# Loading padded inputs in one transfer over 112 partitions, earlier and into five buffers, and letting the state update go through PSUM

## The chip, the cores and the metric

The kernel runs on one core of a Trainium2 chip. The metric is the device time in microseconds of one execution, lower is better. A profile of one execution gives every instruction's start and duration; times in it count from the start of its span.

## What is computed

Three layers follow each other: a gated linear attention over 768 steps, a mixture of 8 experts in which each token goes to its best expert, and a mixture of 4 experts in which each token goes to all of them. The reference, cut to its core:

```
# attention, B=4, H=8, S=768, D=48
for t in range(S):
    state = alpha[:, :, t, :, None] * state + np.einsum('bhd,bhe->bhde', k[:, :, t], v[:, :, t])
    y[:, :, t] = np.einsum('bhd,bhde->bhe', q[:, :, t], state)
...
x = attn_out.transpose(0, 2, 1, 3).reshape(B * S, H * D)
# first mixture, 3072 tokens of 384, 8 experts of 1024
expert_idx = np.argmax(logits, axis=1)
for e in range(E):
    out[mask] = gate_w[mask, None] * (np.maximum(x[mask] @ w1[e], 0.0) @ w2[e])
# second mixture, 4 experts
for e in range(E):
    out += p[:, e:e + 1] * (np.maximum(x @ w1[e], 0.0) @ w2[e])
```

## The kernel before

The attention is cut into 24 units of 128 steps (`NU`); three units make a group `g` of eight (`NG`), and a group's inputs come in two halves `pp`. A unit works on 8 heads at once, two heads on one set of partitions: head rows on partitions 0 to 47 and on 64 to 111 (`R = 112`). Partitions 48 to 63 between them carry padding, so that an instruction can run over all 112.

`load_in(g, pp)` (L353) brings alpha, q and k of a half group into a tile `tin` of 112 partitions and 2311 floats a row (9244 bytes): one transfer for partitions 0 to 47 and one for 64 to 111. There are three such tiles, used in turn (`(2 * g + pp) % 3`), and the padding rows are loaded once into each, by a transfer of 16 rows (L357). So a half group's load waits until the half group three places back has been read for the last time, which is the check of alpha in `prep4` (L418, ScalarE) and the products in `prep2` (L411 and L412).

The work on a half group is: `prep1` with two scans on VectorE, backwards for `G` (L387) and forwards for `bf` (L398); `prep2` with the products with k and q (L411, L412), on GpSimd but for the first group's, which VectorE shares. A unit `u` then goes through `S1` (TensorE: `A` at L432, with the mask applied by VectorE into `At` at L437, and the transposes `kn` at L444), `S2` (TensorE: `y` at L464 and L473, `U` at L485) and `S3` (TensorE: `fin` at L506). At the end of a step the state of the recurrence is updated by VectorE: for the first unit of a sequence by one product (L495), for the next ones by two operations,

```
nc.vector.tensor_tensor(out=sn, in0=pu, in1=so, op=ALU.add)
nc.vector.tensor_tensor(out=sn, in0=sn, in1=bcv, op=ALU.mult)
```

where `pu` is the PSUM tile `U` that TensorE filled, `so` and `sn` are the old and the new state in SBUF (`S`), and `bcv` is a factor in SBUF, spread over the columns. So the first operation reads PSUM and SBUF, the second reads SBUF twice.

The program is written in the order in which it is to run: the scheduler is off (`manual_schedule`), and each engine runs its instructions in the order of the text. A loop over `i` (0 to 28) does S1 of unit i, S3 of unit i-2, S2 of unit i-1, the prep work of coming groups and the routing of finished ones. All loads are issued by SyncE, in order: one whose tile is not yet free holds up all that stand behind it. Besides the inputs these are `v` (L365, 128 partitions), constants (`cst`, `dp`), weights for the mixtures (`wraw`, L60) and `prefill` (L369), eight transfers that write zeros into the memory area `xs` into which the tokens are later scattered by GpSimd (L591).

After the attention the two mixtures run, first with the tokens sorted by expert (windows `xw` of 112 partitions, read back from `xs` at L157), then with all. The change does not touch them. A second program, `general`, is for inputs outside the bounds of the fast one; it is not entered here.

Of the kernel before, what the change touches and what calls it, by code (L numbers as in the profile page):

```python
# [7 lines left out]
F32 = mybir.dt.float32  # L8
# [5 lines left out]
ALU = mybir.AluOpType  # L14
# [3 lines left out]
B, H, S, D = 4, 8, 768, 48  # L18
NT, DM = 3072, 384
E1, E2, FF = 8, 4, 1024  # L20
NFB = FF // 128
KD = DM // 128
NG = 8
CW = 129
# [6 lines left out]
R = 112  # L31
# [276 lines left out]
def attention_and_routing(tc, a, small, keep, xs, info_d, wst, load_w, split_w):  # L308
    nc = tc.nc
# [3 lines left out]
    groups = list(zip([0] + ends[:-1], ends))  # L313
    with ExitStack() as ctx:
        c1 = ctx.enter_context(tc.tile_pool(name="attc", bufs=1))
        vin = ctx.enter_context(tc.tile_pool(name="vin", bufs=2))
        ew = ctx.enter_context(tc.tile_pool(name="ew", bufs=2))
        bd = ctx.enter_context(tc.tile_pool(name="bd", bufs=4))
# [28 lines left out]
        raw = c1.tile([128, NU, 8], F32, name="raw")  # L347
        inf = keep["inf"]

        tbuf = [c1.tile([R, 775 + 1536], F32, name=f"tin{j}") for j in range(3)]  # L350
        tins, vins, qqs, kts, mid = {}, {}, {}, {}, {}

        def load_in(g, pp, lo=0, hi=2311):  # L353
            if (g, pp) not in tins:
                t = tins[g, pp] = tbuf[(2 * g + pp) % 3]
                if 2 * g + pp < 3:
                    nc.sync.dma_start(out=t[D:64, :], in_=a["pad"])  # L357
            for s in range(2):
                nc.sync.dma_start(
                    out=tins[g, pp][64 * s:64 * s + D, lo:hi], in_=a["aqk"][g, pp][s * D:s * D + D, lo:hi]  # L360
                )

        def load_v(g):
            v = vin.tile([128, 3, DM], F32, tag="v", name="v")
# [3 lines left out]
        def prefill(e):  # L368
            nc.sync.dma_start(  # L369
                out=xs[e * NR + LOW:e * NR + W0, :].rearrange("(p j) d -> p j d", j=4),  # L370
                in_=pre[0:(W0 - LOW) // 4, :].unsqueeze(1).to_broadcast([(W0 - LOW) // 4, 4, DM]),
            )
# [81 lines left out]
        def S2(u):  # L454
            g, cl = divmod(u, 3)
            c = u % 6
            At, v = Ats.pop(u), vins[g]
            py = ps1.tile([112, 4, 128], F32, tag="y", name="y")
            for p in range(4):
                for s in range(2):  # L460
                    o = py[0:64, p, :] if s == 0 else py[64:112, p, :]
                    c0 = p * 96 + s * 48
                    n = 64 if s == 0 else 48
                    nc.tensor.matmul(  # L464
                        o, lhsT=v[:, cl, c0:c0 + n], rhs=At[:, s, p, :],
                        start=(p == 0), stop=(c == 0), skip_group_check=True,
                    )
            if c:
                st = Sb[u % 2]
                for p in range(4):  # L470
                    qq = qqs[g, p // 2][:, 2 * cl + p % 2, :]
                    for h in (slice(0, D), slice(64, 64 + D)):
                        nc.tensor.matmul(  # L473
                            py[h, p, :], lhsT=st[h, p], rhs=qq[h], start=False, stop=True, skip_group_check=True
                        )
            yt = wk.tile([112, 4, 128], F32, tag="yt", name="yt")
            nc.scalar.activation(out=yt, in_=py, func=AF.Copy)
            yts[u] = yt
            if c < 5:
                kn = kns.pop(u)  # L480
                pu = ps1.tile([R, 4, D], F32, tag="U", name="U")
                for p in range(4):
                    for h in (slice(0, 64), slice(64, R)):
                        c0 = p * 96 + h.start // 64 * D
                        nc.tensor.matmul(  # L485
                            pu[h, p, :], lhsT=kn[:, p, h], rhs=v[:, cl, c0:c0 + D],
                            start=(p == 0), stop=True, skip_group_check=True,
                        )
                g2, cl2 = divmod(u + 1, 3)

                def state():
                    sn, so = (Sb[(u + j) % 2] for j in (1, 0))
                    bcv = bcall[:, g2, cl2].unsqueeze(2).to_broadcast([R, 4, D])
                    if c == 0:
                        nc.vector.tensor_tensor(out=sn, in0=pu, in1=bcv, op=ALU.mult)  # L495
                    else:
                        nc.vector.tensor_tensor(out=sn, in0=pu, in1=so, op=ALU.add)
                        nc.vector.tensor_tensor(out=sn, in0=sn, in1=bcv, op=ALU.mult)

                late.append(state)  # L500

# [122 lines left out]
        nc.sync.dma_start(out=cst, in_=a["cst"])  # L624
        dp = c1.tile([128, NU, E2], F32, name="dp")
        nc.sync.dma_start(out=dp, in_=a["dp"])
        prefill(0)

        def fill():
            nc.gpsimd.memset(cum, 0.0)  # L630
# [45 lines left out]
        prep2(0, 1, nc.vector, nc.gpsimd, 1, 3)  # L676
        prep_emb2()
        prep4(0, 0)
        load_in(1, 1)
        prep4(0, 1)  # L680

        for i in range(NU + 5):
            for g in range(2, NG):
                if 3 * g - 6 == i:
                    load_in(g, 0)
                if 3 * g - 4 == i:
                    load_in(g, 1)
            for g in range(1, NG):
                if 3 * g - 2 == i:
                    load_v(g)  # L690
            for e in range(E1):
                if e and e - 1 == i:
                    prefill(e)
            if 5 <= i < 27 and i % 2:
                load_w(min((i - 3) // 2, NFB))
            if 0 < i < NU:
                S1(i)
            for g in range(2, NG):
                for pp in range(2):
                    if 3 * g - 3 + pp == i:  # L700
                        prep1(g, pp, part=1)
            if i == 1:
                prep_emb3()
            if 0 <= i - 2 < NU:
                S3(i - 2)
            if 0 <= i - 1 < NU:
                S2(i - 1)
            for r, (u0, u1) in enumerate(groups):
                if i == u1 + 2 and r <= last:
                    route_b(r)  # L710
                if i == u1 + 1:
                    route_a(r)
            for g in range(1, NG):
                for pp in range(2):
                    if max(pp, 3 * g - 4 + pp) == i:
                        prep1(g, pp, part=0 if g > 1 else 2)
                    if 3 * g - 3 + pp == i:
                        prep2(g, pp, nc.gpsimd, nc.gpsimd)
                    if 3 * g - 2 + pp == i:
                        prep4(g, pp)  # L720
            if i == 0:
                fill()
            if i == 2:
                prep_info()
            for r, (u0, u1) in enumerate(groups):
                if i == u1 + 1 and r > last:
                    route_b(r)
                if i == u1 + (3 if r < last else 2 if r == last else 1):
                    route_c(r)
                    scale(r)  # L730
                    if r < last:
                        scatter(r)
                    if r > last:
                        scatter(last)
                        scatter(r)
                        count(r)
            if 6 <= i < 22 and i % 2 == 0:
                split_w((i - 4) // 2)
            while late:
                late.pop(0)()  # L740
# [128 lines left out]
def general(tc, a, ident, out):  # L869

    nc = tc.nc
    with ExitStack() as ctx:
# [7 lines left out]
        with ExitStack() as c1:  # L880
# [4 lines left out]
            with tc.For_i(0, B) as b:  # L885
                for p in range(4):
                    pp, j = divmod(p, 2)
                    al, q, k = (gin.tile([96, S], F32, tag="g" + n, name="g" + n) for n in "aqk")
                    for hf in range(2):
                        src = av[bass.ds(b, 1), hf, pp]  # L890
                        ts = slice(hf * 384, hf * 384 + 384)
                        qk = src[:, :, 775:].rearrange("o p (c z a w) -> (o p) z c a w", c=3, z=2, a=2)[:, :, :, j]
                        ax = src[:, :, 0:774].rearrange("o p (c a w) -> (o p) c a w", c=3, a=2)[:, :, j, 1:CW]
                        for t, x in ((al, ax), (q, qk[:, 0]), (k, qk[:, 1])):
                            nc.sync.dma_start(out=t[:, ts].rearrange("p (c w) -> p c w", w=128), in_=x)
                    for e in range(D):
                        vb = gv.tile([96, S], F32, tag="vb", name="vb")
                        for s in range(2):
# [128 lines left out]
def layout(inputs):  # L1027
# [4 lines left out]
    def pairs(x):  # L1032

        x = x.reshape(B, 2, 2, 2, 2, 3, 128, D)
        return x.transpose(0, 4, 1, 3, 7, 5, 2, 6).reshape(NG, 2, 96, 3, 2, 128)

    aqk = np.zeros((NG, 2, 96, 775 + 1536), np.float32)
    av = np.zeros((NG, 2, 96, 3, 2, CW), np.float32)
    av[..., 1:] = pairs(al)
    aqk[..., 0:774] = av.reshape(NG, 2, 96, 774)  # L1040
    aqk[..., 775:] = np.stack([pairs(q), pairs(k)], axis=4).reshape(NG, 2, 96, 1536)
    pad = np.zeros((16, 775 + 1536), np.float32)
    pad[:, 0:774] = np.arange(774) % CW != 0
    v = np.asarray(inputs["v"]).transpose(0, 2, 1, 3).reshape(NG, 3, 128, DM).transpose(0, 2, 1, 3)

    def unit(w1, w2):
# [10 lines left out]
    for s in range(2):  # L1057
# [17 lines left out]
    cst[:, 640:664] = np.arange(24)[None, :] * 128 + i[:, None]  # L1075
    return {
        "aqk": aqk,
        "pad": pad,
        "v": c(v),
        "wu": c(wu),  # L1080
        "emb": c(inputs["moe_expert_emb"]),
# [28 lines left out]
```

## Time and profile before

| | us |
|---|---|
| median of 3 runs | 1263.68 (1262.91 to 1264.85) |
| the profiled execution, its own time | 1263.84 |
| its span in the profile | 1262.1 |
| TensorE busy over the span | 1188.8 (94%) |
| VectorE busy over the span | 410.2 (33%) |
| GpSimd busy over the span | 324.4 (26%) |

The attention fills roughly the first 215 us; from 222 us on TensorE is busy without a gap. The page of the profile cuts the span into 40 slices of 31.6 us; the first seven are the attention. The engines there are in order: PE is TensorE, DVE VectorE, ACT ScalarE, POOL GpSimd, SP SyncE; "idle before" an instruction is put down to what ended last of that for which it waited.

### The profile page before, as it was taken

What the parts mean: (1) busy time and instruction counts of PE and PEld (TensorE: products, weight loads), DVE (VectorE), ACT (ScalarE), POOL (GpSimd) and SP (SyncE); (2) the same over time, 40 slices, a digit from 0 to 9 for tenths busy, and PEclk for the clock granted to TensorE, in tenths of its full rate; (3) what the DMA queues carried; (4) which work ended last, traced back from release to release, by engine and by line L of the source; (5) the groups of instructions that cost most, each with busy time, mean ns of one, the idle gap of its engine ahead of it and who ended that gap; (6) DMA issues with size and microseconds to landing.
All of it is one profiled execution on the core that took longest, in us unless ns stands there. A gap on an engine that the chain in (4) does not pass through costs nothing.

```text
span 1262.1 us, 17132 instructions
## 1 busy us (share of the span) xinstructions
PE 1188.8 (94%) x7075; PEld 1085.8 (86%) x7075; DVE 410.2 (33%) x752; ACT 328.4 (26%) x605; POOL 324.4 (26%) x220
## 2 busy tenths in 40 slices
PE   4877885999999999999999999999999999999996
PEld 4766674999999999999999999999999999999996
DVE  6887865222322222222222222212222222222221
ACT  2344442444544421111221111131111121111111
POOL 3457562456676620000130000040000021111111
PEclk9887976999999999999999999999999999999998
DMA  8877602644444420000020000020000010000000
GB/s 190 236 179 165 169 29 75 182 131 133 136 136 115 126 65 1 1 1 1 13 89 1 1 1 1 1 75 26 1 1 1 1 39 1 26 25 26 26 25 28
DMA packets 30672, 78.05 MB, mean 62 GB/s; under 512 B 7736, under 2 KB 12088, under 8 KB 29192
## 3 DMA queue, kind: packets, MB, share of 16 engines
q1 hardware_dynamic: 26744, 67.32, 20.1%
q0 software_dynamic: 3840, 9.54, 2.1%
q8 instruction: 57, 0.93, 0.3%
q14 instruction: 31, 0.25, 0.1%
HBM read 63.28 MB, written 13.57 MB: 61 GB/s over the span
## 4 chain that ended last, share of the span: by engine, by line
PE 85%; DVE 5%; issue 4%; DMA 3%; POOL 1%; SPq 1%; ACT 0%; another core or an unknown queue 0%; POOLq 0%; DVEq 0%; ACTq 0%
PE h L123 13%; PE h L125 13%; PE h L124 13%; PE p L272 10%; PE p L271 10%; PE p L270 10%; PE o L212 3%; PE o L211 3%; PE o L213 3%; DMA tin<-in_aqk_dram 2%; PE fin L506 1%; PE A L432 1%; DVE bf L398 1%; DVE At L437 1%; PE y L464 1%
## 5 line engine op out<-in xcount | busy, mean ns | idle before, releaser
L115 DVE SCALAR_TENSOR_TENSOR hl<-h,hh 128x512 fp32r<-128x512 f32 (+8 forms) x264 | 171.9, 651 | 746.0 <-ACT hh L114 738.8
L71 POOL TENSOR_TENSOR wu<-wraw,wu 128x768 fp32r<-128x768 f32 x96 | 180.6, 1883 | 666.8 <-ACT wu L70 666.6
L114 ACT ACTIVATE hh<-h 128x512 fp32r<-128x512 f32 (+8 forms) x264 | 149.5, 566 | 669.8 <-PE h L125 668.1
L272 PE MATMUL p<-wu,hl 128*128 128x384 f32 x768 | 258.8, 337 | 0.0
L271 PE MATMUL p<-wu,hh 128*128 128x384 f32 x768 | 258.2, 336 | 0.0
L270 PE MATMUL p<-wu,hh 128*128 128x384 f32 x768 | 258.0, 336 | 0.0
L123 PE MATMUL h<-x,wu 128*128 128x512 f32 (+1 forms) x600 | 233.0, 388 | 0.0
L125 PE MATMUL h<-x,wu 128*128 128x512 f32 (+1 forms) x600 | 230.6, 384 | 0.0
L124 PE MATMUL h<-x,wu 128*128 128x512 f32 (+1 forms) x600 | 227.9, 380 | 0.0
L271 PEld LDWEIGHTS p<-wu,hh 128*128 128x128 f32 x768 | 144.3, 188 | 7.4
L270 PEld LDWEIGHTS p<-wu,hh 128*128 128x128 f32 x768 | 144.4, 188 | 7.1
L272 PEld LDWEIGHTS p<-wu,hl 128*128 128x128 f32 x768 | 144.3, 188 | 0.0
L125 PEld LDWEIGHTS h<-x,wu 128*128 128x128 f32 x600 | 112.6, 188 | 26.6
L124 PEld LDWEIGHTS h<-x,wu 128*128 128x128 f32 x600 | 112.8, 188 | 16.1
L123 PEld LDWEIGHTS h<-x,wu 128*128 128x128 f32 x600 | 112.8, 188 | 14.5
L70 ACT ACTIVATE wu<-wraw 128x768 fp32r<-128x768 f32 x96 | 80.9, 844 | 80.1 <-PE o L213 38.5
L283 POOL DMA_INDIRECT out_dram<-acc,toki x24 | 23.4, 976 | 183.3 <-DVE acc L279 178.4
L123 PE MATMUL h<-xh,wu 128*128 128x448 f32 (+6 forms) x192 | 70.0, 364 | 0.0
L124 PE MATMUL h<-xh,wu 128*128 128x448 f32 (+6 forms) x192 | 68.1, 354 | 0.0
L125 PE MATMUL h<-xl,wu 128*128 128x448 f32 (+6 forms) x192 | 67.8, 353 | 0.0
L211 PE MATMUL o<-hh,wu 128*128 128x448 f32 (+6 forms) x192 | 67.7, 352 | 0.0
L212 PE MATMUL o<-hl,wu 128*128 128x448 f32 (+6 forms) x192 | 67.6, 352 | 0.0
(148 smaller groups left out, 1103.4 us busy)
## 6 DMA issues: line engine op xcount, KB each, us to landing
wraw<-in_wu_dram SPq DMA_DIRECT2D x96, 384.0 KB, 3.1
tin<-in_aqk_dram SPq DMA_DIRECT2D x28, 433.3 KB, 7.7
xw<-xs SPq DMA_DIRECT2D x7, 672.0 KB, 6.2
v<-in_v_dram SPq DMA_DIRECT2D x8, 576.0 KB, 6.2
xs<-pre SPq DMA_DIRECT2D x8, 480.0 KB, 11.3
tin<-in_aqk_dram SPq DMA_DIRECT2D x4, 192.0 KB, 4.9
xw<-xs SPq DMA_DIRECT2D x3, 224.0 KB, 3.8
tin<-in_pad_dram SPq DMA_DIRECT2D x3, 144.4 KB, 3.2
```

Source lines behind the costliest of these rows:

```text
L70: nc.scalar.activation(out=t[:, 0], in_=r, func=AF.Copy)
L71: nc.gpsimd.tensor_tensor(out=t[:, 1], in0=r, in1=t[:, 0].bitcast(F32), op=ALU.subtract)
L114: nc.scalar.activation(out=hh[:, 0:n], in_=ps, func=AF.Relu)
L115: nc.vector.scalar_tensor_tensor(out=hl[:, 0:n], in0=ps, scalar=0.0, in1=hh[:, 0:n].bitcast(F32), op0=ALU.max, op1=ALU.subtract)
L123: nc.tensor.matmul(ps, lhsT=w[:, 0, ks], rhs=xh(k), start=(k == 0), stop=False)
L124: nc.tensor.matmul(ps, lhsT=w[:, 1, ks], rhs=xh(k), start=False, stop=False)
L125: nc.tensor.matmul(ps, lhsT=w[:, 0, ks], rhs=xl(k), start=False, stop=(k == KD - 1))
L211: nc.tensor.matmul(o, lhsT=w[:, 0, ds], rhs=hh[:, 0:n], start=(f == 0), stop=False)
L212: nc.tensor.matmul(o, lhsT=w[:, 0, ds], rhs=hl[:, 0:n], start=False, stop=False)
L270: nc.tensor.matmul(o, lhsT=hh[:, js], rhs=w[:, 0, DM:2 * DM], start=(f == 0), stop=False)
L271: nc.tensor.matmul(o, lhsT=hh[:, js], rhs=w[:, 1, DM:2 * DM], start=False, stop=False)
L272: nc.tensor.matmul(o, lhsT=hl[:, js], rhs=w[:, 0, DM:2 * DM], start=False, stop=(f == NFB - 1))
```

## The change

Five things are done. The inputs are laid out with the padding in place, 112 rows for each half group, so that one transfer over 112 partitions takes the place of two over 48, and the padding transfers fall away. The tiles come from a pool of five instead of three fixed ones. The loads stand earlier in the text: half group (1,1) at the start, (g,0) at step 3g-8 instead of 3g-6, (g,1) at 3g-6 instead of 3g-4, none before step 0. The eight `prefill` stand at steps 1 to 8 instead of once at the start and at steps 0 to 6. And the state update's first operation leaves its sum in PSUM, in place of `pu`, so that its second reads PSUM and SBUF.

```
-        tbuf = [c1.tile([R, 775 + 1536], F32, name=f"tin{j}") for j in range(3)]
+        tin = ctx.enter_context(tc.tile_pool(name="tin", bufs=5))
...
             if (g, pp) not in tins:
-                t = tins[g, pp] = tbuf[(2 * g + pp) % 3]
-                if 2 * g + pp < 3:
-                    nc.sync.dma_start(out=t[D:64, :], in_=a["pad"])
-            for s in range(2):
-                nc.sync.dma_start(
-                    out=tins[g, pp][64 * s:64 * s + D, lo:hi], in_=a["aqk"][g, pp][s * D:s * D + D, lo:hi]
-                )
+                tins[g, pp] = tin.tile([R, 775 + 1536], F32, tag="tin", name="tin")
+            nc.sync.dma_start(out=tins[g, pp][:, lo:hi], in_=a["aqk"][g, pp][:, lo:hi])
...
-                        nc.vector.tensor_tensor(out=sn, in0=pu, in1=so, op=ALU.add)
-                        nc.vector.tensor_tensor(out=sn, in0=sn, in1=bcv, op=ALU.mult)
+                        nc.vector.tensor_tensor(out=pu, in0=pu, in1=so, op=ALU.add)
+                        nc.vector.tensor_tensor(out=sn, in0=pu, in1=bcv, op=ALU.mult)
...
-        prefill(0)
+        load_in(1, 1)
...
-        load_in(1, 1)
         prep4(0, 1)
...
             for g in range(2, NG):
-                if 3 * g - 6 == i:
+                if max(0, 3 * g - 8) == i:
                     load_in(g, 0)
-                if 3 * g - 4 == i:
+                if max(0, 3 * g - 6) == i:
                     load_in(g, 1)
...
-            for e in range(E1):
-                if e and e - 1 == i:
-                    prefill(e)
+            if 0 < i <= E1:
+                prefill(i - 1)
```

SyncE's queue at the end of the start and in the first steps, before. The names are tile and source; `tin_122` to `tin_124` are the three fixed tiles, the first load here is half group (1,0), then come (1,1), (2,0) and (2,1), each as a pair.

```order
L357 DMA tin_124<-in_pad_dram 16x2311
L359 DMA tin_124<-in_aqk_dram 48x2311 x2
L365 DMA v<-in_v_dram 128x1152
L624 DMA cst<-in_cst_dram 128x736
L626 DMA dp<-in_dp_dram 128x96
L369 DMA xs<-pre 320x1x384
L359 DMA tin_122<-in_aqk_dram 48x2311 x2
L359 DMA tin_123<-in_aqk_dram 48x2311 x2
L369 DMA xs<-pre 320x1x384
L633 DMA info_d<-pre 128x192
L365 DMA v<-in_v_dram 128x1152
```

The same place of the queue in the changed program; the first load is again (1,0).

```order
L356 DMA tin<-in_aqk_dram 112x2311
L360 DMA v<-in_v_dram 128x1152
L619 DMA cst<-in_cst_dram 128x736
L621 DMA dp<-in_dp_dram 128x96
L356 DMA tin<-in_aqk_dram 112x2311 x3
L628 DMA info_d<-pre 128x192
L356 DMA tin<-in_aqk_dram 112x2311
L360 DMA v<-in_v_dram 128x1152
L364 DMA xs<-pre 320x1x384 x2
```

Behind `dp` now stand (1,1), (2,0) and (2,1); the first two need no tile that has been used before, and no `prefill` stands ahead of them. (2,1) and (3,0) wait for the tiles of (0,0) and (0,1).

VectorE's program at the first state update with two operations, before:

```order
L664 TENSOR_TENSOR inf<-dp,ds 128x24x4
L497 TENSOR_TENSOR S_109<-U,S_110 112x192
L498 TENSOR_TENSOR S_109<-S_109,bcall 112x192
L437 TENSOR_TENSOR At<-A_388,ti 128x512
L437 TENSOR_TENSOR At<-A_389,ti 128x512
```

And after the change, where `U` is the tile in PSUM:

```order
L659 TENSOR_TENSOR inf<-dp,ds 128x24x4
L492 TENSOR_TENSOR U<-U,S_113 112x192
L493 TENSOR_TENSOR S_112<-U,bcall 112x192
L432 TENSOR_TENSOR At<-A_379,ti 128x512
L432 TENSOR_TENSOR At<-A_380,ti 128x512
```

Nothing moves on VectorE: the 16 pairs keep their places and change an operand each. TensorE, ScalarE and GpSimd run the same instructions in the same order as before.

## Rows read from the trace of the kernel before

**Rows 1.** The page: span, busy tenths of PE, DVE and DMA in 40 slices.

```profile
span 1262.1 us, 17132 instructions
...
PE   4877885999999999999999999999999999999996
...
DVE  6887865222322222222222222212222222222221
...
DMA  8877602644444420000020000020000010000000
```

**Rows 2.** Chain that ended last: start us, us, what; the DMA pieces of `tin`.

```profile
17.89 14.38 DMA tin<-in_aqk_dram
...
55.73 7.92 DMA tin<-in_aqk_dram
```

**Rows 3.** Timeline, 0 to 60 us: start, us, engine, line [idle before <-releaser].

```profile
0.73 0.40 SPq L357 DMA_DIRECT2D tin<-in_pad_dram  x1
...
1.19 1.80 SPq L359 DMA_DIRECT2D tin<-in_aqk_dram  x4
...
4.58 0.70 DVE L387 TENSOR_TENSOR_SCAN G<-tin,dind 112x258 f32<-112x258 f32 x1 [2.78 <-DMA tin<-in_aqk_dram]
...
13.16 0.69 DVE L411 TENSOR_TENSOR bf<-tin,bf 112x512 f32<-112x512 f32 x1 [0.95 <-DMA tin<-in_aqk_dram]
...
22.87 1.77 DVE L387 TENSOR_TENSOR_SCAN G<-tin,dind 112x774 f32<-112x774 f32 x1 [1.83 <-DMA tin<-in_aqk_dram]
...
26.59 1.26 DVE L437 TENSOR_TENSOR At<-A,ti 128x512 f32<-128x512 f32 x2
...
26.76 1.68 POOL L411 TENSOR_TENSOR bf<-tin,bf 112x768 f32<-112x768 f32 x1 [9.30 <-DVE bf L398]
...
28.39 1.68 POOL L412 TENSOR_TENSOR G<-tin,G 112x768 f32<-112x768 f32 x1
...
32.37 1.77 DVE L387 TENSOR_TENSOR_SCAN G<-tin,dind 112x774 f32<-112x774 f32 x1 [4.42 <-DMA tin<-in_aqk_dram]
```

**Rows 4.** Stretches; the last two columns are the DMA engines' busy share and GB/s.

```profile
13.50:22.00 8.50, 3.81 (x24) 3.00 (x24) 7.13 (x15) 2.22 (x5) 2.58 (x2) 1.00 1.02 161
22.50:25.00 2.50, 1.08 (x10) 1.08 (x12) 2.06 (x3) 0.32 (x2) 0.00 (x0) 1.00 1.03 396
...
131.50:136.50 5.00, 4.75 (x72) 3.98 (x72) 4.93 (x7) 1.45 (x4) 3.24 (x2) 1.00 0.95 172
137.50:139.30 1.80, 0.76 (x14) 0.52 (x10) 1.73 (x4) 1.34 (x3) 1.80 (x2) 1.00 0.95 373
250.50:254.00 3.50, 3.50 (x19) 3.19 (x18) 0.63 (x1) 1.20 (x3) 1.66 (x2) 1.00 0.91 258
```

**Rows 5.** Who waited for whom, DMA queue: total us, times, longest us.

```profile
SPq L359 <- ACT ajunk L418: 57.5, 9, 10.5
```

**Rows 6.** The state update by line: count, ns min/median/max, first and last start.

```profile
L498 DVE TENSOR_TENSOR S<-S,bcall x16: 357/358/4283, 42.6 to 200.9; 112x192 f32<-112x192 f32 x16
...
L497 DVE TENSOR_TENSOR S<-U,S x16: 317/358/358, 42.2 to 200.5; 112x192 f32<-112x192 f32 x16
```

**Rows 7.** Timeline, 60 to 160 us, columns as in Rows 3.

```profile
63.77 2.38 DVE L387 TENSOR_TENSOR_SCAN G<-tin,dind 112x774 f32<-112x774 f32 x1 [0.99 <-DMA tin<-in_aqk_dram]
...
90.43 1.34 DVE L498 TENSOR_TENSOR S<-S,bcall 112x192 f32<-112x192 f32 x1
...
103.96 4.28 DVE L498 TENSOR_TENSOR S<-S,bcall 112x192 f32<-112x192 f32 x1
104.58 1.69 POOL L412 TENSOR_TENSOR G<-tin,G 112x768 f32<-112x768 f32 x1
...
106.32 1.23 PE L432 MATMUL A<-bf,G 48*128 48x128 f32 x8 [3.75 <-POOL G L412]
...
138.19 1.33 DVE L498 TENSOR_TENSOR S<-S,bcall 112x192 f32<-112x192 f32 x1
...
148.44 5.75 DVE L387 TENSOR_TENSOR_SCAN G<-tin,dind 112x774 f32<-112x774 f32 x1
```

More of the change, by code (lines that the diff above doesn't have):

```diff
@@ L894, in general @@
                         for t, x in ((al, ax), (q, qk[:, 0]), (k, qk[:, 1])):
-                            nc.sync.dma_start(out=t[:, ts].rearrange("p (c w) -> p c w", w=128), in_=x)
+                            for s in range(2):
+                                nc.sync.dma_start(
+                                    out=t[s * D:s * D + D, ts].rearrange("p (c w) -> p c w", w=128),
+                                    in_=x[64 * s:64 * s + D],
+                                )
                     for e in range(D):
@@ L1035, in pairs @@
         return x.transpose(0, 4, 1, 3, 7, 5, 2, 6).reshape(NG, 2, 96, 3, 2, 128)
[L1037 to L1043, printed above, removed]
+    aqk = np.zeros((NG, 2, R, 775 + 1536), np.float32)
+    rows = np.r_[0:D, 64:64 + D]
+    av = np.ones((NG, 2, R, 3, 2, CW), np.float32)
+    av[..., 0] = 0.0
+    av[:, :, rows, :, :, 1:] = pairs(al)
+    aqk[..., 0:774] = av.reshape(NG, 2, R, 774)
+    aqk[:, :, rows, 775:] = np.stack([pairs(q), pairs(k)], axis=4).reshape(NG, 2, 96, 1536)
     v = np.asarray(inputs["v"]).transpose(0, 2, 1, 3).reshape(NG, 3, 128, DM).transpose(0, 2, 1, 3)
@@ L1077, in layout @@
         "aqk": aqk,
-        "pad": pad,
         "v": c(v),
```

## The prediction

> **What bounds the kernel now.** I read the page first [rows 1]. TensorE shows a 9 in nearly every slice from the eighth on, and 4 to 8 in the seven slices of the attention. The change touches the attention alone, so it can win or lose only there, in some 215 us; what it wins moves everything behind it forward by the same time. In the attention VectorE stands at 6 to 8 tenths, TensorE at 4 to 8: neither is full, so time goes where one waits for another. The DMA engines start at 8 and fall to 4 and less.
>
> Then the chain of waits [rows 2]. It holds two long pieces in which a load of `tin` is what all wait for: 14.38 us up to 32.3 us and 7.92 us up to 63.7 us. Not all of that is waiting, since VectorE worked beside it. What VectorE lost is the idle time before its instructions in the timeline [rows 3, 7]: 2.78 us before 4.58, 0.95 before 13.16, 1.83 before 22.87, 4.42 before 32.37 and 0.99 before 63.77. There is none behind that: from 64 us on no load of `tin` is late.
>
> Why the loads are late is seen in two further views. In the DMA queue, SyncE stood 57.5 us in all in front of a `tin` load until ScalarE's check had released its tile [rows 5]. And while loads of `tin` run, the DMA engines are full but move little: 161 GB/s from 13.5 to 22 us and 172 GB/s from 131.5 to 136.5 us, at shares of 1.02 and 0.95. With `v` and the constants (128 partitions) they move 396 and 373 GB/s at the same shares [rows 4].
>
> **The change, part by part.** A half group was two times 48 rows of 9244 bytes, 0.887 MB; it becomes 112 rows, 1.035 MB. The three padding transfers go (3 x 0.148 MB), which is what the first three tiles gain, so up to (1,0) the bytes are the same.
>
> *The transfer's rate.* No row shows a 112-row load of `tin`. The nearest is `xw`, 112 rows of 6144 bytes, in the stretch at 250.5 us: 258 GB/s, with some weights beside it; the upper end is 373 GB/s, `v` at 128 rows [rows 4]. So a load costs the DMA engines 1.035/373 = 2.8 to 1.035/258 = 4.0 us, against 0.887/172 = 5.2 now. I reckon with the slow end, since it is 112 rows too.
>
> The Trainium skill has two rules here that speak against each other. Its page "SBUF — State Buffer", section "Door 1: The DMA port swizzle", says that a transfer's partitions decide how many of 16 ports it can use, and that partitions 0 to 63 reach only half of them; 172 against 373 GB/s agrees with that. Its page "DMA: Bandwidth & Descriptors", section "Anatomy of one DMA — SWDGE (gpsimd) path", gives a DMA's time as about 2 us and its bytes over 436 GB/s, by which the new load would be dearer, by an estimate of 0.34 us (0.148 MB more). By the first the sum stays as it is worked out below; by the second the four loads up to (1,1) would cost 1.4 us more than now, and only the earlier issue would win anything, which is the first rival.
>
> *The start.* Now the first scan waits for three issues, from 0.73 us (padding) to the second half at some 1.65, and starts at 4.58, 2.9 us after the last [rows 3]. With one issue at 0.73 it starts at 3.7: 0.9 us. The wait of 0.95 at 13.16 is for a piece that stands behind 16 issues now, some 0.46 us apart, and behind eight after the change; it goes: 0.95 us.
>
> *Half groups (1,0) and (1,1).* The queue up to (1,1) then holds four half groups (4.14 MB), `ti`, `v`, `cst` and `dp` (1.15 MB): 5.29 MB, at 258 GB/s 20.5 us. With the first landing at 3.7 us, (1,1) is there at 24.2 at the latest; (1,0), with 3.24 MB up to it, at 16.3. VectorE will want (1,0) at 22.87 - 0.9 - 0.95 - 1.83 = 19.2 and (1,1) at 32.37 - 8.1 = 24.3. Both waits go, the second only just at the slow rate: 1.83 + 4.42 = 6.25 us.
>
> *What meets there instead.* Now GpSimd runs two products at 26.76 and 28.39, while VectorE, done with `At` at 27.85, waits for its data until 32.37 [rows 3]. After the change VectorE comes to its scan while the first of these runs. Both read SBUF twice, and scans that come in the midst of a GpSimd product last longer: 2.38 us at 63.77, 5.75 at 148.44 instead of some 1.77 [rows 7]. So VectorE will stand until the first product ends (28.44 - 27.85 = 0.6 us) or the second (30.07 - 27.85 = 2.2). Rows show both kinds; I take the middle, 1.4 us lost.
>
> *The load of (3,0).* The 0.99 us at 63.77 [rows 7] go: with five tiles it is issued at step 1, four steps ahead of its scan, when (0,1) has long been read. 0.99 us.
>
> *The state update.* The first operation reads PSUM and SBUF and takes at most 358 ns in all 16 cases. The second reads SBUF twice; its median is 358 too, but up to 4283 ns [rows 6]. The three longest are 1.34, 4.28 and 1.33 us [rows 7]. With PSUM as one source the second should hold to the first one's time. At 90.43 and 138.19 VectorE goes on at once with masks and a scan, so 0.98 + 0.97 = 1.95 us come off its path. At 103.96 the excess is 3.92 us, but the second half of `A` waits for GpSimd's product until 106.32 whatever VectorE does, and TensorE's work follows from there: I count nothing, 3.9 at most. That the first operation now writes PSUM is shown by no row, since only TensorE does that here. Below, it costs nothing; above, as much again as the operation, 16 x 0.36 = 5.7 us. I take nothing, as reading PSUM adds nothing measurable.
>
> *Costed at nothing.* `prefill` moves from the start to steps 1 to 8. The last stands behind half group (5,0) and `v`; both wait for work of step 6 at most, and the scatter that it must precede is in step 9, with some 8 us to a step; if it were late, GpSimd would stand with two products behind it. SyncE's waits for tiles stay, but the tile of five places back is read two steps and more before, so nothing behind a load comes too late; `v` and weights are the ones to be held up. The longer `general` is not entered.
>
> **The sum.** 0.9 + 0.95 + 6.25 - 1.4 + 0.99 + 1.95 = 9.6 us. The profiled execution's own time, 1263.84, lies 0.16 above the median of 1263.68. 1263.84 - 9.6 = 1254.2, so against the median some 1254.0.
>
> **The rivals.**
> *The bytes decide, not the partitions.* Then four half groups at 172 GB/s take 24.1 us and the rest at 396 GB/s 2.9, and (1,1) lands at 30.7, not at 24.2. At 32.37 only 1.7 us are won in place of 8.1 - 1.4; with 0.99 and 1.95 that is 4.6 us: 1259.2. Against it stands that 128 rows run at twice the rate at the same share of the engines [rows 4].
> *Who gets SBUF first.* The scan at 148.44 stood 4.0 us behind GpSimd's products. All times shift by unequal amounts, so that VectorE may come first there, or may come second elsewhere. Each such case is worth 4.0: 1250.2 without it, 1258.2 with one more.
> *TensorE takes over.* In slices two to four it is at 8, 7 and 7 tenths [rows 1]. If it can't follow when VectorE stops waiting, half of the lead is lost: about 1259.
> *Writing PSUM is slow (slower).* It decides from (9.6 + 2.5)/16 = 0.76 us a step on VectorE's path, when the operation would take three times its 358 ns. At four times, 1.07 us, it is 17.2 - 9.6 = 7.6 us of loss: 1271. For it speaks only that no row shows it; against it, that reading PSUM is as quick as reading SBUF.
>
> **How the numbers follow.** A measurement of this kernel tells a change from none from about 0.2%, 2.5 us. Chances: the forecast 0.52, the long stall gone 0.12, one more of it 0.10, bytes decide 0.11, TensorE 0.08, PSUM 0.04, no gain for a reason that I don't see 0.03. The first five are faster, but for some 0.05 that falls short; so 0.88 faster, 0.07 the same, 0.05 slower. The range reaches down to the long stall gone with 103.96 counted in part (1247.5), and up to where the load rate stays and little else comes (1260).
>
> **What would show it.** Right: a `tin` load moves 260 GB/s or more; no idle time of VectorE for `tin` behind the first; the scan of (1,1) at 24 to 27 us; all 16 second operations under 0.4 us; the attention's end some 10 us earlier. Wrong: loads still at 170 GB/s; a first operation above 0.5 us; TensorE waiting as long as before at the scatter; a stall like that at 148.44 at a new place.

## The result and the profile after

The changed kernel takes 1253.16 us (median of 4 runs, 1249.73 to 1254.57), the kernel before 1263.3 us (4 runs): ratio 0.9915, 95% interval 0.9891 to 0.9938. The forecast was 1254.0 us, faster, with a range of 1247.5 to 1260. The profiled execution took 1254.57 us, its span is 1252.4 us, 9.7 us less than before; the forecast's terms add up to 9.6.

The page of the changed kernel, the slices that answer to [rows 1]:

```profile
span 1252.4 us, 17070 instructions
...
PE   4988785999999999999999999999999999999996
...
DVE  8876655222222222222222222222122222222221
...
DMA  9964214444443410000120000020000010000000
```

In the first slice VectorE is at 8 tenths where it was at 6. In the fourth and fifth slice the DMA engines are at 4 and 2 where they were at 7 and 6: the loads are done sooner.

A stretch of the changed kernel, the last two columns again the DMA engines' share and GB/s, against the first of [rows 4]:

```profile
13.50:22.00 8.50, 5.26 (x50) 4.47 (x48) 8.02 (x15) 3.02 (x8) 1.18 (x1) 1.00 1.02 289
```

From 13.5 to 22 us the loads move 289 GB/s in place of 161 at the same share, but not the same loads. By the sizes of the packets, the stretch of before holds (1,0) and 51 packets of `v`; that of the changed kernel holds the rest of (1,0), all 128 packets of `v`, the constants and loads of `tin` behind them. For the shape alone, stretches count in which nothing but `tin` moves: before from 27 to 33 us, in the changed kernel from 22.5 to 26 us, here in this order:

```profile
27.00:33.00 6.00, 6.00 (x40) 5.42 (x41) 1.58 (x4) 0.45 (x2) 3.53 (x5) 1.00 0.97 159
```

```profile
22.50:26.00 3.50, 3.13 (x34) 2.72 (x35) 2.66 (x5) 0.79 (x2) 3.40 (x4) 1.00 1.03 275
```

There `tin` moves at 275 GB/s in place of 159.

The timeline of the changed kernel, columns as in [rows 3, 7] (the lines of the code have moved up by 5, so L382 is the scan that was L387):

```profile
2.96 0.70 DVE L382 TENSOR_TENSOR_SCAN G<-tin,dind 112x258 f32<-112x258 f32 x1 [1.16 <-DMA tin<-in_aqk_dram]
...
10.93 0.69 DVE L406 TENSOR_TENSOR bf<-tin,bf 112x512 f32<-112x512 f32 x1 [0.45 <-DMA tin<-in_aqk_dram]
...
18.74 1.75 DVE L382 TENSOR_TENSOR_SCAN G<-tin,dind 112x774 f32<-112x774 f32 x1
...
24.23 1.68 POOL L407 TENSOR_TENSOR G<-tin,G 112x768 f32<-112x768 f32 x1
...
24.64 2.90 DVE L382 TENSOR_TENSOR_SCAN G<-tin,dind 112x774 f32<-112x774 f32 x1 [0.84 <-DMA tin<-in_aqk_dram]
...
43.07 0.37 DVE L492 TENSOR_TENSOR U<-U,S 112x192 f32<-112x192 f32 x1 [1.40 <-PE U L480]
...
57.25 1.76 DVE L382 TENSOR_TENSOR_SCAN G<-tin,dind 112x774 f32<-112x774 f32 x1
...
60.32 3.43 DVE L393 TENSOR_TENSOR_SCAN bf<-tin,dfw 112x774 f32<-112x774 f32 x1
...
60.45 1.67 POOL L407 TENSOR_TENSOR G<-tin,G 112x768 f32<-112x768 f32 x1
...
68.79 1.29 DVE L432 TENSOR_TENSOR At<-A,ti 128x512 f32<-128x512 f32 x2 [2.39 <-PE A L427]
...
94.62 0.37 DVE L492 TENSOR_TENSOR U<-U,S 112x192 f32<-112x192 f32 x1 [2.41 <-PE U L480]
95.02 0.36 DVE L493 TENSOR_TENSOR S<-U,bcall 112x192 f32<-112x192 f32 x1
...
98.93 1.29 DVE L432 TENSOR_TENSOR At<-A,ti 128x512 f32<-128x512 f32 x2 [3.55 <-PE A L427]
...
136.93 1.76 DVE L382 TENSOR_TENSOR_SCAN G<-tin,dind 112x774 f32<-112x774 f32 x1
...
142.40 1.69 POOL L407 TENSOR_TENSOR G<-tin,G 112x768 f32<-112x768 f32 x1
...
144.14 1.23 PE L427 MATMUL A<-bf,G 48*128 48x128 f32 x8 [4.09 <-POOL G L407]
...
145.40 0.69 DVE L432 TENSOR_TENSOR At<-A,ti 128x512 f32<-128x512 f32 x1 [5.08 <-PE A L427]
...
152.91 1.29 DVE L432 TENSOR_TENSOR At<-A,ti 128x512 f32<-128x512 f32 x2 [2.55 <-PE A L427]
```

Read against [rows 3, 7]: the first scan stands 1.62 us earlier, the `bf` product 2.23, the scan of (1,0) 4.13. The scan of (1,1) starts 7.73 us earlier, but waits 0.84 us for its data and then lasts 2.90 us beside GpSimd's product, so it ends 6.60 us earlier (34.14 to 27.54). At 43.07 VectorE waits for TensorE, and 5.45 us of the lead are left. The scan of (3,0) ends 7.14 us earlier and waits for nothing. Behind it a scan is new that stands by a GpSimd product, at 60.32.

The state update by line, as in [rows 6], the first step and the second:

```profile
L492 DVE TENSOR_TENSOR U<-U,S x16: 341/366/367, 36.1 to 190.3; 112x192 f32<-112x192 f32 x16
...
L493 DVE TENSOR_TENSOR S<-U,bcall x16: 357/357/359, 36.5 to 190.7; 112x192 f32<-112x192 f32 x16
```

No second step is above 359 ns; the first, which now writes PSUM, has a median of 366 where it was 358. SyncE's waits for ScalarE's check, to set against [rows 5]:

```profile
SPq L356 <- ACT ajunk L413: 48.7, 8, 9.1
```

They are 8.8 us shorter in all, and behind the scan of (1,1) VectorE waits for no load of `tin` any more.

### The profile page after: what moved, and what is told of

Same layout as the page of the kernel before. It is cut to its first block, busy times and chain, and to the rows that moved or that the text cites. A ratio compares the mean times of both kernels' runs of the same rounds, so it can differ in the third digit from the quotient of the medians.

```text
span 1252.4 us, 17070 instructions
## 1 busy us (share of the span) xinstructions
PE 1185.6 (95%) x7075; PEld 1082.6 (86%) x7075; DVE 398.9 (32%) x752; ACT 327.7 (26%) x605; POOL 323.6 (26%) x220
## 4 chain that ended last, share of the span: by engine, by line
PE 82%; issue 3%; DMA 1%; DVE 1%; POOL 1%; ACT 0%; SPq 0%; ACTq 0%; POOLq 0%
PE h L123 13%; PE h L125 13%; PE h L124 13%; PE p L272 10%; PE p L271 10%; PE p L270 10%; PE o L212 3%; PE o L213 3%; PE o L211 3%; PE xt L178 1%; PE fin L501 1%; DMA wraw<-in_wu_dram 1%; PE y L459 1%; PE A L427 1%; PE y L468 1%
```

## The experiments

Three series of four kernels, each series on a chip of its own, each kernel beside the kernel before.

| chip, before | kernel | us | ratio, 95% interval |
|---|---|---|---|
| first, 1253.11 | state update alone | 1252.84 | 0.9994 (0.9983 to 1.0005) |
| | loads alone | 1248.09 | 0.9956 (0.9940 to 0.9972) |
| | two transfers a load | 1250.01 | 0.9970 (0.9954 to 0.9986) |
| | shape alone | 1247.87 | 0.9958 (0.9942 to 0.9974) |
| second, 1264.15 | changed kernel | 1251.51 | 0.9897 (0.9881 to 0.9913) |
| | kernel before | 1263.96 | 0.9999 (0.9988 to 1.0011) |
| | old places | 1252.51 | 0.9909 (0.9894 to 0.9923) |
| | 128 rows | 1252.33 | 0.9906 (0.9892 to 0.9921) |
| third, 1263.86 | old rows | 1266.9 | 1.0030 (1.0015 to 1.0044) |
| | state update alone | 1260.54 | 0.9967 (0.9954 to 0.9980) |
| | loads alone | 1256.61 | 0.9939 (0.9922 to 0.9957) |
| | changed kernel | 1252.97 | 0.9907 (0.9888 to 0.9925) |

**The state update alone (first chip).** The kernel before with

```diff
-                        nc.vector.tensor_tensor(out=sn, in0=pu, in1=so, op=ALU.add)
-                        nc.vector.tensor_tensor(out=sn, in0=sn, in1=bcv, op=ALU.mult)
+                        nc.vector.tensor_tensor(out=pu, in0=pu, in1=so, op=ALU.add)
+                        nc.vector.tensor_tensor(out=sn, in0=pu, in1=bcv, op=ALU.mult)
```

> The kernel before, with only the state update's second step reading PSUM (loads, tiles and prefill as before). By the forecast's term 0.98 + 0.97 = 1.95 us come off: about 1261.5 against 1263.4, all 16 second operations at 0.4 us or less, the first ones at 0.36 to 0.37 us as in the changed kernel. Rival, the excess of the second operation lies beside other waits: no change. Rival, what stood behind GpSimd's products goes on standing there at the next operation with two SBUF sources: the second operation is short, and a scan, a mask or At within 3 us behind it is longer by 1 us or more, no change.

Measured: 0.3 us less, not told from none. All second steps are at 357 to 359 ns, the first ones at 334 to 367. So writing PSUM costs no more than some 8 ns a step, and on this chip the shorter second steps bring nothing that can be measured. The kernel before took 10 us less here than on the chip of the result, so the term had to be tried again on another.

**The loads alone (first chip).** The changed kernel with the same four lines turned back.

> The changed kernel with the old state update (both steps write SBUF, the second reads SBUF twice). By the forecast the loads alone give 9.6 - 1.95 = 7.65 us, so 1255 to 1256, second operations above 1 us come back at three places or so, and the first scan of (1,1) starts at about 24.6 as in the changed kernel. Rival, the state update gives nothing: 1253.2, as the changed kernel. Rival, most of the gain is the state update's: 1259 or more.

Measured: 5.0 us less than before. Six second steps are over 1 us again, one of 4.80. That is less than the 7.65 of the forecast. How much of the whole change it is on this chip is not known, since the changed kernel was not run there.

**Two transfers a load (first chip).** The changed kernel with

```diff
-            nc.sync.dma_start(out=tins[g, pp][:, lo:hi], in_=a["aqk"][g, pp][:, lo:hi])
+            for ps in (slice(0, 64), slice(64, R)):
+                nc.sync.dma_start(out=tins[g, pp][ps, lo:hi], in_=a["aqk"][g, pp][ps, lo:hi])
```

> The changed kernel, but each load is issued as two transfers, partitions 0 to 63 and 64 to 111, with the same bytes, tiles and places. If the spread over partitions sets the rate (the forecast): 160 to 180 GB/s from 13.5 to 22 us as before the change, the scan of (1,1) waits until 29 to 31 us in place of 24.6, and the time is 1257.5 to 1260. Rival, the earlier issue and five tiles bring the gain and the spread brings nothing: 260 GB/s or more, 1253 to 1254. Rival, only the number of issues counts: the start is later by 0.5 us and nothing else.

Measured: 227 GB/s from 13.5 to 22 us, more than the forecast and less than with one transfer (255 and 296 in the two other traces of 112-row transfers on this chip). Where only `tin` moves it is 208 (25 to 33 us), against 219 in both others (22.5 to 26 us); from 3 to 9 us it is 158, against 206 and 222. The scan of (1,1) stands at 31.16 us after a wait of 3.96. The time is 3.1 us less than before, where the loads alone give 5.0. That lies between the two theories: 64 and 48 rows do better than 48 and 48. The traced execution is one of the quickest of this kernel (1246.69 us; they go from 1245.5 to 1256.15). In it the loads alone are ahead by 4.65 us at the `At` of 73.69 (69.04 there), and by nothing at the one of 174.79 (174.88): what is lost at the start can be won back before the attention ends.

**The shape alone (first chip).** The kernel before with one transfer of 112 rows a half group, everything else old:

```diff
-            for s in range(2):
-                nc.sync.dma_start(
-                    out=tins[g, pp][64 * s:64 * s + D, lo:hi], in_=a["aqk"][g, pp][s * D:s * D + D, lo:hi]
-                )
+            nc.sync.dma_start(out=tins[g, pp][:, lo:hi], in_=a["aqk"][g, pp][:, lo:hi])
```

> The kernel before, with only its loads as one transfer over 112 partitions (three fixed tiles, the old places of the loads and of prefill, the old state update). If the shape of the transfer brings the gain: 1255 to 1257, no more than 1 us above the changed kernel with the old state update, idle time of VectorE for a load of tin at most 1.5 us in all behind the start. Rival, the places of the issue and the five tiles are needed: (1,1) is issued behind the steps of (0,1) as before and waits some 4 us as before, 1259 to 1261.

Measured: the same as the loads alone (0.9958 and 0.9956). `tin` kept VectorE waiting for 4.0 us behind the start, more than the 1.5 expected, but for the same 3.7 us with the loads alone. Places, five tiles and the moved prefill bring nothing that can be told; the shape brings it.

**The changed kernel and the kernel before again (second chip).** No edits.

> The changed kernel as it is, since on the chip of the first four experiments the kernel before took 1253.1 us, 10 us less than on the chip of the first comparison. If the change is worth what its terms are worth on any chip: 8.5 to 10 us less than before on this chip, too, ratio 0.992 to 0.993, so 2 to 4 us below the changed kernel with the old state update. Rival, what the loads win is all that is left on this chip (the state update alone gave 0.3 us there): 5 to 6 us less than before, ratio 0.995 to 0.996.

> The kernel before as it is, for its trace on this chip. Ratio 1.000. If the 10 us between the chips come from the attention's end: the stretch from At at 183.3 us to the last fin lasts 11 to 14 us in place of 22, TensorE runs through U there without stops of 0.5 to 1.2 us, its granted clock stays 1.00 in that stretch, and up to there both traces agree within 3 us. Rival, the whole attention is slower by parts on the one chip: they lie 5 us or more apart before 160 us already.

Measured: the gain is there again, 12.6 us between the medians. This chip is like that of the result (before takes 1264.15 us), so the stretch at the attention's end lasts 22.3 us again; the first chip shows 13.9. Its trace, that of the state update alone, since one of the kernel before is missing there, stands at 160.06 us with the `At` that stands at 159.18 here. So of the 10 us between the chips 8.4 lie at the attention's end, as the first theory has it, so far as the state update alone can stand for the kernel before. TensorE of the kernel before in its last step but one, on this chip:

```profile
186.17 0.59 PE L485 MATMUL U<-v,kn_s 128*64 128x48 f32 x4
187.26 0.20 PE L485 MATMUL U<-v,kn_s 128*64 128x48 f32 x1 [0.50 <-issue]
187.99 0.25 PE L485 MATMUL U<-v,kn_s 128*64 128x48 f32 x2 [0.53 <-issue]
189.43 0.45 PE L485 MATMUL U<-v,kn_s 128*48 128x48 f32 x3 [1.19 <-issue]
190.14 0.24 PE L485 MATMUL U<-v,kn_s 128*48 128x48 f32 x1 [0.26 <-issue]
190.85 0.47 PE L485 MATMUL U<-v,kn_s 128*48 128x48 f32 x5 [0.47 <-issue]
```

and its whole end from there, the third number from the right the granted clock:

```profile
182.80:205.10 22.30, 18.47 (x184) 15.26 (x185) 10.03 (x49) 8.12 (x22) 8.15 (x9) 0.77 0.19 72
```

The same place with the state update alone on the first chip, where before and that kernel take the same time:

```profile
184.09 0.67 PE L485 MATMUL U<-v,kn_s 128*64 128x48 f32 x16
```

```profile
180.70:194.60 13.90, 13.20 (x186) 11.47 (x185) 9.84 (x49) 8.09 (x22) 8.06 (x9) 1.00 0.31 115
```

The 16 products take 5 us in place of 0.67 because TensorE stops between them for nothing that the profile shows. From the end of the third stop its clock is granted at 1.2 GHz for some 10 us (0.50 below), where the other trace has 1.00 through the whole stretch, and the same work takes 22.3 us in place of 13.9. That the stops bring the lower clock is likely by their order and not shown by a run.

```profile
189.50:199.40 9.90, 9.17 (x74) 7.56 (x76) 3.48 (x13) 1.95 (x6) 0.86 (x2) 0.50 0.06 22
```

In the changed kernel the stops are there too on the chip of the result (2.9 us in five waits), so they cancel in the comparison.

The load of (1,1) differs from one execution of the changed kernel to the next. Here:

```profile
13.50:22.00 8.50, 4.69 (x32) 3.83 (x34) 8.02 (x16) 2.50 (x7) 1.46 (x2) 1.00 1.03 261
```

```profile
27.78 1.77 DVE L382 TENSOR_TENSOR_SCAN G<-tin,dind 112x774 f32<-112x774 f32 x1 [2.85 <-DMA tin<-in_aqk_dram]
```

It waits 2.85 us in place of 0.84, but then does not stand beside GpSimd (1.77 in place of 2.90), and the span is 1251.0 us, 1.4 less than in the profile above.

**Old places (second chip).** The changed kernel with

```diff
-        load_in(1, 1)
...
+        load_in(1, 1)
         prep4(0, 1)
...
-                if max(0, 3 * g - 8) == i:
+                if 3 * g - 6 == i:
                     load_in(g, 0)
-                if max(0, 3 * g - 6) == i:
+                if 3 * g - 4 == i:
                     load_in(g, 1)
```

> The changed kernel with the loads back at their old places: (1,1) behind the first steps, the others two steps later; five tiles, one transfer of 112 rows, prefill and state update as changed. If the transfer's rate brings the gain and not the places: the same as the changed kernel within 1.5 us, idle time of VectorE for a load behind the start at most 3 us in all. Rival, the places bring it: (1,1) waits 3.5 us or more, 3 us or more above the changed kernel.

Measured: 1.0 us above the changed kernel, the intervals of the two ratios overlap; (1,1) waits 1.51 us, idle time for a load 2.2 us in all behind the start. As with the shape alone, the places bring nothing that can be told.

**128 rows (second chip).** The changed kernel with 16 zero rows more:

```diff
-        tins, vins, qqs, kts, mid = {}, {}, {}, {}, {}
+        full, tins, vins, qqs, kts, mid = {}, {}, {}, {}, {}, {}
...
-                tins[g, pp] = tin.tile([R, 775 + 1536], F32, tag="tin", name="tin")
-            nc.sync.dma_start(out=tins[g, pp][:, lo:hi], in_=a["aqk"][g, pp][:, lo:hi])
+                full[g, pp] = tin.tile([128, 775 + 1536], F32, tag="tin", name="tin")
+                tins[g, pp] = full[g, pp][0:R]
+            nc.sync.dma_start(out=full[g, pp][:, lo:hi], in_=a["aqk"][g, pp][:, lo:hi])
...
-    aqk = np.zeros((NG, 2, R, 775 + 1536), np.float32)
+    aqk = np.zeros((NG, 2, 128, 775 + 1536), np.float32)
```

> The changed kernel with 16 zero rows more to each load: 128 partitions, 1.183 MB in place of 1.035 MB, same places and tiles. If the spread over partitions sets the rate: 373 to 396 GB/s as with v, a load takes 3.0 to 3.2 us in place of 3.6, what is left of the wait before the scan of (1,1) goes, 0 to 1 us faster than the changed kernel. Rival, bytes set the time at some 290 GB/s for any row count: 4.1 us a load, the scan of (1,1) waits 1 to 2 us longer than in the changed kernel, and the time is 0.5 to 2 us above it.

Measured:

```profile
13.50:22.00 8.50, 5.26 (x47) 4.47 (x47) 8.02 (x15) 2.87 (x8) 1.18 (x1) 1.00 1.03 426
```

```profile
23.87 2.19 DVE L383 TENSOR_TENSOR_SCAN G<-tin,dind 112x774 f32<-112x774 f32 x1
...
24.40 3.14 POOL L408 TENSOR_TENSOR G<-tin,G 112x768 f32<-112x768 f32 x1
...
26.32 2.84 DVE L394 TENSOR_TENSOR_SCAN bf<-tin,dfw 112x774 f32<-112x774 f32 x1
```

All loads in this stretch have 128 rows. Against the stretch from 22.5 to 26 us of the two traces above from this chip, in which only `tin` moves (227 and 248 GB/s), 14% more bytes come at 1.7 to 1.9 times the rate, and (1,1) waits for no data. The time is the same as the changed kernel's (0.8 us above it, intervals overlapping): VectorE now meets GpSimd's product in two scans, which last 2.19 and 2.84 us in place of 1.77, and GpSimd's product 3.14 in place of 1.68. The loads are no longer what bounds this stretch.

**Old rows (third chip).** The changed kernel with

```diff
-            nc.sync.dma_start(out=tins[g, pp][:, lo:hi], in_=a["aqk"][g, pp][:, lo:hi])
+            for ps in (slice(0, D), slice(D, 64), slice(64, R)):
+                nc.sync.dma_start(out=tins[g, pp][ps, lo:hi], in_=a["aqk"][g, pp][ps, lo:hi])
```

> The changed kernel, but each load in three transfers with the old rows: partitions 0 to 47, 48 to 63 (the padding) and 64 to 111; bytes, tiles, places, prefill and state update as changed. If the shape of the transfer sets its rate: 160 to 200 GB/s from 13.5 to 22 us, the scan of (1,1) starts at 31 us or later, and the time is 3 to 6 us above the changed kernel's 0.990 to 0.992 of before, so a ratio of 0.994 or more. Rival, the earlier issue brings the gain whatever the rate: within 1.5 us of the changed kernel.

Measured:

```profile
13.50:22.00 8.50, 2.53 (x17) 2.05 (x18) 7.08 (x15) 2.27 (x5) 3.75 (x2) 1.00 1.08 188
```

```profile
24.44 1.77 DVE L383 TENSOR_TENSOR_SCAN G<-tin,dind 112x774 f32<-112x774 f32 x1 [2.11 <-DMA tin<-in_aqk_dram]
...
34.25 1.77 DVE L383 TENSOR_TENSOR_SCAN G<-tin,dind 112x774 f32<-112x774 f32 x1 [4.73 <-DMA tin<-in_aqk_dram]
```

All of the change but the shape of the transfer, and the kernel is 3.0 us slower than before, 13.9 slower than the changed kernel: the waits of [rows 3] are back, and the padding's bytes and issues come on top. VectorE's idle time for `tin` behind the first scan is 12.4 us, where it was 8.2 before and is 1.3 in the profile above. The 13.9 us are more than twice the 3 to 6 that were expected; where the rest comes from was not followed up.

**Each half and both (third chip).** The first two kernels of the first series and the changed kernel, no further edits.

> The state update alone once more, in one call with the loads alone and with both. Where TensorE stops in U at the attention's end as in the first traces: 1.95 us less than before, ratio 0.9985, if the term holds; ratio 1.000 (as the 0.9994 on the other chip) if what VectorE wins it waits for elsewhere.

> The loads alone once more. If the terms add: 7.65 us and more less than before, ratio 0.992 to 0.994, and 1.5 to 3 us above both together. Rival, the loads alone give as much as both: the same as the changed kernel within 1 us.

> The changed kernel, beside its two halves on the same chip. Before takes 1263 to 1264 us here (TensorE stops in U at the attention's end): ratio 0.990 to 0.992. Before takes 1253 us: the gain is that of the loads alone there, ratio 0.995 to 0.996, if the state update stays at 0.3 us.

Measured: 3.3, 7.3 and 10.9 us less than before. The halves add up (10.6). Where the state update's part is: the scan that stood for 5.75 us in [rows 7] stands for 4.50 with the loads alone,

```profile
141.53 1.71 POOL L407 TENSOR_TENSOR G<-tin,G 112x768 f32<-112x768 f32 x1
...
142.14 4.50 DVE L382 TENSOR_TENSOR_SCAN G<-tin,dind 112x774 f32<-112x774 f32 x1
...
147.20 1.28 DVE L432 TENSOR_TENSOR At<-A,ti 128x512 f32<-128x512 f32 x2
```

and with the state update alone it doesn't stand, but the next `At` waits:

```profile
143.41 1.76 DVE L387 TENSOR_TENSOR_SCAN G<-tin,dind 112x774 f32<-112x774 f32 x1
...
147.98 0.36 DVE L498 TENSOR_TENSOR S<-U,bcall 112x192 f32<-112x192 f32 x1
...
148.88 1.69 POOL L412 TENSOR_TENSOR G<-tin,G 112x768 f32<-112x768 f32 x1
...
151.37 1.29 DVE L437 TENSOR_TENSOR At<-A,ti 128x512 f32<-128x512 f32 x2 [3.03 <-PE A L432]
```

## Why the prediction was right

**The transfer's shape.** The step that carries the sum holds, at a lower rate than was taken. Where only `tin` moves, 112 rows in one transfer reach 219 to 275 GB/s in seven traces (22.5 to 26 us; 275, 227 and 222 in the three of the changed kernel), and 48 rows 156 to 171 in four traces of the old loads (27 to 33 us). The 258 that the prediction called the slow end is above six of the seven; it comes from a stretch in which weights of 128 rows moved beside `xw`. The rival "the bytes decide" falls by the old rows (13.9 us slower at the same bytes) and by 128 rows (more bytes, a higher rate). The other half of that rival, that the earlier issue would win anything, falls by the old places. The 1.4 us that the rule on bytes was to cost were too many in any case: three of the four loads up to (1,1) had their padding loaded before, too.

**The waits.** The start is 2.23 us earlier by the `bf` product, not 1.85, since the first piece lands 2.2 us behind its issue and not 3; 0.45 of the wait there is left. (1,0): as reckoned, the wait of 1.83 is gone. (1,1): "at 24.2 at the latest" was too early. It came at 24.64 in one trace and at 27.4 to 27.8 in the two others of the changed kernel, since the queue does not move 258 GB/s from its first byte (220 GB/s from 3 to 9 us in the quickest of the three) and in those two not later either. The 1.4 us set aside for GpSimd came out as 0.84 of wait and 1.13 of meeting in one, as 2.85 of wait and no meeting in the next: data late or GpSimd busy, one stands in for the other, and 128 rows give both back as meetings. The end of that scan, 6.60 us earlier, is what the terms made of it (6.7) in the profile above alone; in the two other traces it is 4.6 and 4.9, against the same trace of before.

**(3,0).** 0.99 us of wait and 0.62 of a long scan are gone, and the next scan pays 1.64 of it (3.43 us at 60.32; the one of before took 1.79). The term is nil in the end; the prediction did not see that the meeting only moves on by one operation. A further 0.72 us of the lead are lost at 43.07, where VectorE now waits 1.40 us for TensorE's `U` in place of 0.68: the rival "TensorE takes over", in small.

**The state update.** The two steps of 1.34 and 1.33 us gave the 0.98 and 0.97 that were reckoned. The one of 4.28 was counted as nothing, and its shortening by itself gives 0.29: VectorE reaches the next `At` 9.23 us earlier, and stood 8.94 earlier already at the first operation of that step. The 1.56 us between that and the 7.38 of the steps ahead of it come from a shorter wait before that operation, 2.41 us in place of 3.97; for what ended the wait of before the profile names no engine ("remote"). Lines of before:

```profile
74.35 1.29 DVE L437 TENSOR_TENSOR At<-A,ti 128x512 f32<-128x512 f32 x2 [2.44 <-PE A L432]
...
103.56 0.36 DVE L497 TENSOR_TENSOR S<-U,S 112x192 f32<-112x192 f32 x1 [3.97 <-remote]
...
108.16 1.27 DVE L437 TENSOR_TENSOR At<-A,ti 128x512 f32<-128x512 f32 x2
...
154.75 1.28 DVE L437 TENSOR_TENSOR At<-A,ti 128x512 f32<-128x512 f32 x2
...
159.61 1.26 DVE L437 TENSOR_TENSOR At<-A,ti 128x512 f32<-128x512 f32 x2
```

At the `At` of 122.63 (130.21 before) 0.2 of all this was left; a scan of 3.14 us at 107.27, where the one of before took 2.48, is part of the rest. The term was 1.95; alone the state update measured 3.3 us on the third chip and 0.3 on the first. PSUM's price, taken as nil, is 8 ns.

**The long stall at 148.44.** The forecast left it where it was, the rival gave 4.0 us for its end. It is gone in all nine traces with the state update on PSUM. It is gone in two of the three traces of the old state update with new loads, too; there a second operation stands for 3.4 us instead. Yet in the profile above its end does not give 4.0 us. The `At` pair two steps ahead of it (139.45 before, 130.78 now) is 8.67 us earlier, the pair behind it (154.75, 145.40) 9.35, and the next (159.61, 152.91) 6.70. GpSimd's products are issued behind its transfers all the same, TensorE needs them for `A` (it waits 4.09 us for that at 144.14), and `At` waits 5.08 us at 145.40 for `A`. A wait of VectorE behind GpSimd became a wait for what GpSimd makes.

**The sum was right in part by luck.** Behind all terms of the loads, at the `At` of 68.79 (74.35 before), the lead is 5.56 us in the profile above, and 4.6 and 4.9 in the two other traces of the changed kernel, against the same trace of before; the terms up to there make 7.69. From there to the end of the attention the lead grows to 9.9 us (10.8 and 8.5 in the others), where the sum had 1.95 left. So the loads gave less than reckoned by that point, and what followed gave more, in meetings and waits that no term names. The two misses nearly cancel. The loads alone, on the third chip, show that this is not the state update's doing: 5.2 us at that `At`, 7.6 at the end of the attention.

**The signs.** Of what was to show the forecast right, the second operations (359 ns at most) and the end of the attention came as said. 260 GB/s is reached in one trace of the changed kernel out of three; VectorE's idle time for `tin` behind the first scan is 1.3, 4.6 and 4.3 us and not nil; the scan of (1,1) starts at 24.64, 27.78 and 27.44 us. Of the signs of being wrong, loads at 170 GB/s and a first operation above 0.5 us (367 ns at most) stayed away. TensorE waits for `xw` behind the scatter as long as before (1.79 us, 1.76 before), but 9.9 us earlier, so that sign said nothing; and the wait of 5.08 us at 145.40 is a stall at a new place, though not one of VectorE behind GpSimd itself.

**What stays open.** Why TensorE stops in `U` in every trace of the result and of the second and third chip, and in none of the first, was not tried; no load of code falls among the stops (in the trace shown they lie between 186.8 and 190.9 us, and pieces of the instruction queue start at 179.61 and 192.84). Nor is it shown why the first chip gives the loads only 5.0 us and the state update 0.3: the changed kernel and the trace of before are missing there. What its traces show is that the loads' lead over the state update alone is 7.7 us at the `At` of 160.06 (152.34 with the loads) and 5.9 us at the end of the attention.

The Trainium skill, page "SBUF — State Buffer", section "Who interferes with whom", states that a VectorE instruction with at most one SBUF input does not contend with GpSimd, and that one with two does with a GpSimd instruction that reads SBUF. The trace agrees: 32 steps of the state update with PSUM as one source, none over 367 ns; with two SBUF sources up to 4283.

## What to carry to other kernels

When a load keeps the DMA engines full and moves little, look at how many partitions one transfer covers before moving its issue: padding rows that let one transfer cover 112 partitions were worth more than all places and buffers together. Where two engines meet over SBUF, price a removed wait by what the waiting engine needs next, not by its own length: the end of 4 us of stall was worth 0.7 at the next step and nothing at the one behind it. Add up the lead at several places along the kernel, not only at its end: a sum can meet the total though its terms miss. Split a change into its halves on one chip, and run the whole beside them, since chips differ by as much as the change.

## What the runs showed of the hardware

Where only loads of one shape move, transfers of 48 rows reach 156 to 171 GB/s, of 112 rows 219 to 275, of 128 rows 426. The Trainium skill's page "SBUF — State Buffer", section "Door 1: The DMA port swizzle", gives 16 ports of 8 partitions, and of partitions 0 to 47 some ports serve all 8. If the fullest port sets the time, 48 rows take as long as 128, by an estimate 48/128 x 426 = 160 GB/s; the trace agrees. For 112 rows the same estimate gives 373, and the traces show a quarter to four tenths less: the fullest port alone does not explain it, and why is open.

TensorE stopped 0.25 to 1.2 us at a time between 16 small products, at the same place of the program in every trace but those of the first chip; with a granted clock of 0.50 for some 10 us behind the third stop, the stretch took 8.4 us longer, of 1260.
